# Fused attention and four-expert layer on one core: the second expert with seven half-size products in five pairs of token tiles instead of seven, and three vector operations moved

## The chip, the cores and the metric

The kernel runs on one core of one Trainium2 chip. The metric is the device time of one execution in microseconds (us). Before the change the median of three runs is 383.03 us (382.89 to 383.79). The profiled execution, from which all the lines of the profile come, has a span of 381.7 us. The engines are named as the profile names them: PE is the matrix engine (PEld its weight loads), DVE the vector engine, ACT the scalar engine, POOL and SP the two that mostly issue transfers.

## What is computed

The first half is attention for 4 batches, 8 heads, 768 positions and a head size of 64. Three of the heads look at all earlier positions, five only at 4 first positions and a window of 64. The result, seen as 3072 tokens of 512 values, goes through four dense experts whose outputs are added with the weights `p`:

```python
def _moe_ref(x, domain_probs, w1, w2):       # x: 3072 x 512
    p = domain_probs / (domain_probs.sum(-1, keepdims=True) + 1e-09)
    out = np.zeros((N, D))
    for e in range(E):                       # E = 4, hidden size 1024
        h = np.maximum(x @ w1[e], 0.0)
        out += p[:, e:e+1] * (h @ w2[e])
    return out
```

## The kernel before, in words

The 3072 tokens are 24 tiles of 128. The first four tiles go through the experts one expert after the other. The other twenty are taken as ten *pairs* of tiles, called here by the number of the first tile: pair 4, 6, 8 and so on to 22. Each pair is one call of `pair_steps(nt0, nxt)`, where `nxt` is the next pair.

**Layer one of a pair.** The token inputs of each expert are first multiplied by that expert's weight `p` (`scale_inputs`, L1111; one operation of 128x1024 elements, or two of 128x512 where the pair straddles two attention chunks). The products can then be added over the experts with no further scaling. An expert's first layer is done in one of two ways:

- `plain_layer1`: 32 matmuls with 256 columns (L1155) and four ReLUs on ACT (L1164);
- `winograd_layer1`: a Strassen-Winograd scheme with seven products of half size in each direction, which is 56 matmuls with 128 columns (L1184). It needs sums of the inputs (`scaled_sums`, L1125 and L969, and one more subtraction in place on the quarter `x_part(e, 0, 1)`), three copies to `kept` on ACT (L1194), three additions with ReLU on DVE (L1201) and one ReLU on ACT (L1234). It also needs sums of the weights, made once for each expert (`first_weight_sums`).

`EW = (3, 2)` names the experts that may be done in the second way. Expert 3 is done so in every pair. Expert 2 is done so only where `two(nt0)` holds, in the last `LAST` pairs. With `LAST = 7` these are pairs 10 to 22, and the weight sums of expert 2 are made in pair 8. A table called `order` in `pair_steps` says how the steps of the plain experts (`n`) and of the two others (`a` for expert 3, `b` for expert 2) follow each other and which DVE operation stands behind which group of steps.

**Layer two of a pair.** It is the same seven-product scheme over all four experts at once: seven products of 16 matmuls with 256 columns (L1287), in the order A11, A12, S2, S1, S3, S4, A22. The sums S2, S3 and S4 (each two halves of 128x1024 elements, L969) are made on DVE between them. Two accumulators in PSUM, `x` and `y`, are emptied by ACT copies (L1307) and DVE additions (L1310, `add`). Behind the products S3, S4 and A22 also stand the scalings and input sums of the *next* pair. If the next pair does expert 2 in the second way, the flag `ahead` holds, and the scalings of experts 3, 0 and 2 stand there. Otherwise only those of experts 0 and 3 do, and expert 2 is scaled in the middle of the next pair's layer one.

**Attention between the pairs.** Everything is issued by one program in a fixed order for each engine. The loop at the end draws a step from `moe_steps()`, adds its nominal time to `spent`, and puts in attention steps for a later chunk of tokens when `spent` has passed what `plan` gives. So each engine's queue holds a mixture: score products (L660) and value products (L714, L786) on PE, exponentials (L678) and the logarithm and exponential of a reciprocal (L804, L814) on ACT, mask products (L682), normalisation (L809, L739 to L743) and copies of keys (L290, L274) on DVE. The last three pairs have no attention beside them.

Of the kernel before, what the change touches and what calls it, by code (L numbers as in the profile page):

```python
# [19 lines left out]
def kernel(  # L20
# [80 lines left out]
    def bank():  # L101
        return pA.tile([P, 512], FP32, name="pA", bufs=4)
# [11 lines left out]
    EW = (E - 1, E - 2)  # L114
# [422 lines left out]
    def mm_ns(cols):  # L537
        return cols / 2.4 + 2.5
# [429 lines left out]
    def minus(out, a, b):  # L968
        nc.vector.tensor_tensor(out=out, in0=a, in1=b, op=ALU.subtract)  # L969
# [9 lines left out]
    def w1_part(e, j, k):  # L979
        c = e * DMP + j * KH  # L980
        return w1sb[:, c : c + KH, k * FN : (k + 1) * FN]
# [3 lines left out]
    def first_weight_sums(e):  # L985

        return [
            lambda: minus(t1[e, 0], w1_part(e, 0, 1), w1_part(e, 0, 0)),
            lambda: minus(t1[e, 1], w1_part(e, 1, 1), t1[e, 0]),
            lambda: minus(t1[e, 2], w1_part(e, 1, 0), t1[e, 1]),  # L990
            lambda: minus(w1_part(e, 0, 1), w1_part(e, 1, 1), w1_part(e, 0, 1)),
        ]
# [81 lines left out]
    def pieces(nt0):  # L1074

        g0, j0 = divmod(nt0, 3)
        n0 = min(3 - j0, PT)
        yield g0, j0 * P, 0, n0
        if n0 < PT:
            yield g0 + 1, 0, n0, PT - n0  # L1080
# [12 lines left out]
    def scaled(e):  # L1093
        if e in own_room:
            return own_room[e]
        n = 2 if e == EW[0] else e % 2
        x = xs_of[0][:, n * DMP * PC : (n + 1) * DMP * PC]
        return x.rearrange("p (c x) -> p c x", c=DMP)

    def scale_inputs(nt0, e):  # L1100

        if xs_of[0] is None:
            xs_of[0] = moe.tile([P, XS], FP16, name="xs", tag="xs", bufs=1)
        xs = scaled(e)
        for g, c0, t0, n in pieces(nt0):
            require(g)
            xin = xT[g][:, :, c0 : c0 + n * P].rearrange("p c (t x) -> p c t x", t=n)
            o = xs[:, :, t0 * P : (t0 + n) * P].rearrange("p c (t x) -> p c t x", t=n)
            pb = pB_of[nt0][:, t0 : t0 + n, e, :]
            pb = pb.rearrange("p t (c x) -> p c t x", c=1)  # L1110
            nc.vector.tensor_tensor(  # L1111
                out=o, in0=xin, in1=pb.to_broadcast([P, DMP, n, P]), op=ALU.mult
            )

    def x_part(e, i, j):
        return scaled(e)[:, j * KH : (j + 1) * KH, i * P : (i + 1) * P]

    def x_sum(n):

        n0 = WT * NSH * P + n * KH * P  # L1120
        return kSf[:, n0 : n0 + KH * P].rearrange("p (c x) -> p c x", c=KH)

    def scaled_sums(e):

        nc.vector.tensor_tensor(  # L1125
            out=x_sum(0), in0=x_part(e, 1, 0), in1=x_part(e, 1, 1), op=ALU.add
        )
        minus(x_sum(1), x_sum(0), x_part(e, 0, 0))
        minus(x_part(e, 1, 0), x_part(e, 0, 0), x_part(e, 1, 0))
# [9 lines left out]

    PSHARE = 1.57  # L1140

    LAST = 7

    def two(nt0):
        return nt0 >= pairs[-LAST]

    def pair_steps(nt0, nxt):
# [29 lines left out]
        def winograd_layer1(e, x, y):  # L1177

            ns = HT * KH * mm_ns(P)

            def product(ps, w, a, first):
                for f in range(HT):
                    for ct in range(KH):
                        nc.tensor.matmul(  # L1184
                            out=ps[:, f * P : (f + 1) * P],
                            lhsT=w[:, ct, f * P : (f + 1) * P],
                            rhs=a[:, ct, :],
                            start=(first and f == 0 and ct == 0),
                            stop=(ct == KH - 1),
                            skip_group_check=True,  # L1190
                        )

            def keep(n, ps):
                nc.scalar.copy(out=kept[n], in_=ps)  # L1194

            def block(n):
                return blocks[:, n, e * HT : (e + 1) * HT, :]

            def add(n, ps, b):

                nc.vector._custom_dve(  # L1201
                    TENSOR_ADD_SAT,
                    out=block(b),
                    in0=ps.rearrange("p (f x) -> p f x", f=HT),
                    in1=kept[n].rearrange("p (f x) -> p f x", f=HT),
                    s0=LARGEST,
                    s1=0.0,
                )

            def t(n):  # L1210
                return t1[e, n]

            product(x, w1_part(e, 0, 0), x_part(e, 0, 0), True)
            keep(0, x)
            yield ns, 0.5
            z = bank()
            product(z, w1_part(e, 1, 0), x_part(e, 0, 1), True)
            add(0, z, 0)
            yield ns, 0.5
            product(x, t(1), x_sum(1), False)  # L1220
            keep(1, x)
            yield ns, 0.5
            product(y, t(0), x_sum(0), True)
            keep(2, y)
            minus(x_part(e, 0, 1), x_part(e, 0, 1), x_sum(1))
            yield ns, 0.5
            product(x, w1_part(e, 0, 1), x_part(e, 1, 0), False)
            add(2, x, 3)
            yield ns, 0.5
            product(y, w1_part(e, 1, 1), x_part(e, 0, 1), False)  # L1230
            add(1, y, 2)
            yield ns, 0.5
            product(x, t(2), x_part(e, 1, 1), False)
            nc.scalar.activation(  # L1234
                out=block(1), in_=x.rearrange("p (f x) -> p f x", f=HT), func=AF.Relu
            )
            yield ns, 0.5

        a, b = (winograd_layer1(e, *y) for e, y in zip(EW, (banks, banks[::-1])))

        more = []
        if nt0 == pairs[-LAST - 1]:
            more = first_weight_sums(EW[1])
# [39 lines left out]
        def product(ps, a, b, first, middle=None):  # L1285
            for k in range(KT):
                nc.tensor.matmul(  # L1287
                    out=ps,
                    lhsT=a[:, k, :],
                    rhs=b(k),  # L1290
                    start=(first and k == 0),
                    stop=(k == KT - 1),
                    skip_group_check=not first,
                )
                if k == KT // 2 - 1:
                    if middle is not None:
                        middle()
                    yield KT // 2 * mm_ns(HN), PSHARE

        def b(k, n):  # L1300
            return lambda kt: whole_b(k, n, kt // HT, kt % HT)
# [4 lines left out]
        def keep(n, ps):  # L1306
            nc.scalar.copy(out=s[:, n, :], in_=ps)  # L1307

        def add(n, ps, i, j):
            nc.vector.tensor_tensor(  # L1310
                out=o[:, i, j * HN : (j + 1) * HN], in0=ps, in1=s[:, n, :], op=ALU.add
            )

        def store(i, j=None):
            r = slice((nt0 + i) * P, (nt0 + i + 1) * P)
            c = slice(0, DM) if j is None else slice(j * HN, (j + 1) * HN)
            nc.sync.dma_start(out=out[r, c], in_=o[:, i, c])

        def second_sum(n):
            k = slice(n * KT // 2, (n + 1) * KT // 2)  # L1320
            minus(S2[:, k, :], S1[:, k, :], A11[:, k, :])
# [11 lines left out]
        ahead = nxt and two(nxt)  # L1333
# [3 lines left out]
        yield from product(x, A11, b(0, 0), True)  # L1337
        keep(0, x)
        second_sum(0)
        yield half  # L1340
        yield from product(y, A12, b(1, 0), True, lambda: second_sum(1))
        add(0, y, 0, 0)
# [12 lines left out]
        add(2, x, 1, 1)  # L1355
        if last:
            keep(3, x)
        else:
            scale_inputs(nxt, 0)
        yield half  # L1360
        yield from product(
            y, S4, b(1, 1), False, lambda: scaled_sums(EW[0]) if ahead else None
        )
        add(1, y, 0, 1)
        if nxt is not None:
            scale_inputs(nxt, EW[1] if ahead else EW[0])
        store(0)
        if last:
            store(1, 1)
# [18 lines left out]
            return  # L1388
        yield from product(x, A22, t(2), False)
        nc.scalar.copy(out=o[:, 1, 0:HN], in_=x)  # L1390
        if not ahead:
            scaled_sums(EW[0])
        if more:
            more[3]()
# [91 lines left out]
    def require(a):  # L1486
        drained = False
        while state["a"] <= a:
            attention_step()
            drained = True  # L1490
        if drained:
            tick(LAG)
        while any(g <= a for _, _, g in behind):
            behind.pop(0)[1]()
# [48 lines left out]
```

The softmax here doesn't subtract the row's maximum and nothing guards it: scores larger than these inputs give would overflow.

## Time and profile before

| what | value |
|---|---|
| device time, median of 3 | 383.03 us |
| span of the profiled run | 381.7 us |
| PE busy | 368.1 us (96%), 4224 matmuls |
| DVE busy | 283.2 us (74%) |
| ACT busy | 227.6 us (60%) |
| POOL busy | 111.5 us (29%) |
| granted PE clock | 1.00 throughout |

The pairs begin at 88.3 us. The busy time of an engine is a sum of its records. A matmul's record runs from its start to its modelled end (272 ns for 256 columns), while the next one starts long before that. So PE counts as busy as long as one matmul follows another, and the time that PE loses shows as a small gap in that share. The `idle` bracket of a timeline line is the gap in front of it, with the engine and line whose event ended it. Since the record in front covers the latency of the last matmul, the true loss at such a place is about 0.16 us more than the bracket: 272 ns of a record less the 109 ns at which such matmuls follow each other.

### The profile page before, as it was taken

The numbers are of one execution on the slowest core, as the hardware profiler recorded it, in microseconds if no ns is written. First come the engines' busy times: TensorE is split into PE (matmuls) and PEld (weight loads), VectorE is DVE, ScalarE is ACT, GpSimd is POOL, SyncE is SP. The second block draws the span as 40 slices with busy tenths as digits, with TensorE's granted clock in tenths as the row PEclk, the third lists the DMA queues.
The fourth block names the chain that finished last, engine by engine and source line by source line (L and its number), as shares of the span: only waits on it lengthen the run. The fifth ranks groups of instructions, "written<-read, shape, count | busy, mean of one in ns | idle before, by whom it ended". The sixth has DMA issues, their size and how long they took to land.

```text
span 381.7 us, 10324 instructions
## 1 busy us (share of the span) xinstructions
PE 368.1 (96%) x4224; PEld 310.8 (81%) x4224; DVE 283.2 (74%) x617; ACT 227.6 (60%) x475; POOL 111.5 (29%) x154
## 2 busy tenths in 40 slices
PE   8889999999999999999999899799999999999996
PEld 4754466678998988998889798798998999998996
DVE  6774768797797689979679869957957956857562
ACT  3863479547776785775666756665677362360630
POOL 8925563961066048027302550210000000000000
PEclk9999999999999999999999999999999999999999
DMA  9999999999799299899906991961220110300101
GB/s 167 153 204 204 197 192 179 179 206 85 109 108 160 77 103 148 142 99 79 169 12 74 180 121 26 116 125 14 61 78 2 55 58 2 112 3 2 58 0 57
DMA packets 124772, 39.25 MB, mean 103 GB/s; under 512 B 113728, under 2 KB 118404, under 8 KB 124724
## 3 DMA queue, kind: packets, MB, share of 16 engines
q0 software_dynamic: 86848, 19.01, 58.8%
q1 hardware_dynamic: 36276, 19.18, 22.2%
q8 instruction: 33, 0.54, 0.6%
q10 hardware_dynamic: 1600, 0.39, 0.5%
q14 instruction: 15, 0.12, 0.1%
HBM read 44.89 MB, written 6.34 MB: 134 GB/s over the span
## 4 chain that ended last, share of the span: by engine, by line
PE 81%; DVE 12%; ACT 4%; issue 2%; DVEq 0%; ACTq 0%
PE pO L1287 25%; PE pA L1155 19%; PE pO L1184 10%; PE pA L1026 7%; PE pO L1047 7%; PE pA L660 4%; DVE xs L1111 2%; PE pA L1184 2%; PE pV L714 2%; ACT rc L804 2%; PE pV L786 1%; DVE xT L809 1%; DVE hA L969 1%; PE pO L430 1%; DVE es L682 1%
## 5 line engine op out<-in xcount | busy, mean ns | idle before, releaser
L1287 PEld LDWEIGHTS <-hA 128*128 128x128 f16 x1104 | 104.9, 98 | 13.7 <-issue 1.3
L1164 ACT ACTIVATE hA<-pA 128x512 f16<-128x512 f32 x92 | 55.0, 598 | 37.0 <-PE pA L1155 35.1
L1287 PE MATMUL pO<-w2sb,hA 128*128 128x256 f16 x640 | 76.7, 272 | 0.3 <-DVE hA L1201 0.2
L678 ACT ACTIVATE es<-pA 128x384 f16<-128x384 f32 (+2 forms) x122 | 59.0, 511 | 28.4 <-PE pA L660 24.0
L1155 PEld LDWEIGHTS <-w1sb 128*128 128x128 f16 x736 | 68.7, 98 | 6.9
L1155 PE MATMUL pA<-xs,w1sb 128*128 128x256 f16 x512 | 64.6, 273 | 0.0
L306 POOL DMA_DIRECT2D vS<-in_v_dram x30 | 29.6, 987 | 117.1 <-PE pV L786 113.5
L1287 PE MATMUL pO<-tsb,hA 128*128 128x256 f16 x464 | 56.8, 272 | 0.7 <-DVE o L1310 0.7
L1111 DVE TENSOR_TENSOR xs<-xT,pB 128x1024 f16<-128x1024 f16 (+1 forms) x43 | 40.8, 969 | 0.0
L969 DVE TENSOR_TENSOR hA<-hA 128x1024 f16<-128x1024 f16 x60 | 39.7, 685 | 0.4
L1184 PEld LDWEIGHTS <-w1sb 128*128 128x128 f16 x544 | 33.8, 98 | 5.5 <-issue 3.0
L1039 ACT ACTIVATE hA<-pA 128x384 f16<-128x384 f32 (+1 forms) x64 | 22.2, 385 | 19.8 <-PE pA L1026 19.6
L1184 PE MATMUL pO<-xs,w1sb 128*128 128x128 f16 x408 | 30.6, 219 | 3.3 <-DVE o L1310 1.1
L1026 PE MATMUL pA<-xT,w1sb 128*128 128x384 f16 (+1 forms) x256 | 30.9, 273 | 1.4 <-DVE xT L767 1.3
L1201 DVE CUSTOM_DVE_ANT_0 hA<-pO,s 128x512 f16<-128x512 f32 x34 | 23.1, 689 | 12.2 <-ACT s L1194 6.5
L1194 ACT COPY s<-pO 128x512 f32<-128x512 f32 x51 | 29.4, 588 | 4.0 <-PE pO L1184 2.7
L1047 PE MATMUL pO<-w2sb,hA 128*128 128x512 f16 x128 | 30.7, 379 | 0.0
L1155 PE MATMUL pA<-hA,w1sb 128*128 128x256 f16 x224 | 29.0, 273 | 0.0
L1026 PEld LDWEIGHTS <-w1sb 128*128 128x128 f16 x256 | 19.4, 98 | 10.2 <-issue 1.9
L1307 ACT COPY s<-pO 128x256 f32<-128x256 f32 x31 | 11.6, 373 | 26.5 <-PE pO L1287 19.3
L1184 PEld LDWEIGHTS <-t1sb 128*128 128x128 f16 x408 | 25.9, 98 | 1.1 <-issue 0.2
L804 ACT ACTIVATE rc<-pV,eps 64x384 f32<-64x384 f32 x37 | 21.3, 576 | 8.0 <-PE pV L786 7.4
(138 smaller groups left out, 526.8 us busy)
## 6 DMA issues: line engine op xcount, KB each, us to landing
pB<-p_rows SPq DMA_DIRECT2D x10, 512.0 KB
out_dram<-o SPq DMA_DIRECT2D x19, 256.0 KB
w1sb<-in_moe_w_dram POOLq DMA_DIRECT2D x8, 512.0 KB, 9.2
w2sb<-in_moe_w_dram POOLq DMA_DIRECT2D x4, 1024.0 KB, 12.2
vS<-in_v_dram POOLq DMA_DIRECT2D x30, 112.0 KB, 4.6
k_rows<-in_k_dram POOLq DMA_DIRECT2D x18, 128.0 KB, 5.1
q<-in_q_dram POOLq DMA_DIRECT2D x18, 128.0 KB, 6.2
vR<-in_v_dram POOLq DMA_DIRECT2D x24, 48.0 KB, 5.4
```

The costliest lines, as they stand in the source:

```text
L306: gp.dma_start(out=t[:, :, own_v(h)], in_=windows_of(v, b, h, c))
L678: nc.scalar.activation(out=es[:, 0:cols], in_=ps[:, 0:cols], func=AF.Exp, scale=SC)
L804: nc.scalar.activation(out=rc[r, :], in_=ps[o, 0:CH], func=AF.Ln, bias=eps[o, :])
L969: nc.vector.tensor_tensor(out=out, in0=a, in1=b, op=ALU.subtract)
L1026: nc.tensor.matmul(out=pss[ft][:, 0:cols_n], lhsT=w1sb[:, e * DMP + ct, ft * P : (ft + 1) * P], rhs=x[:, ct, :], start=(n == 0), stop=(n = ...
L1047: nc.tensor.matmul(out=ps_o, lhsT=hs[:, ft, j * P : (j + 1) * P], rhs=w2sb[:, e * FTP + ft, :], start=(ft == 0), stop=(ft == FTP - 1),)
L1111: nc.vector.tensor_tensor(out=o, in0=xin, in1=pb.to_broadcast([P, DMP, n, P]), op=ALU.mult)
L1155: nc.tensor.matmul(out=ps[:, f * PC : (f + 1) * PC], lhsT=w1sb[:, e * DMP + ct, (f0 + f) * P : (f0 + f + 1) * P], rhs=xs[:, ct, :], start= ...
L1164: nc.scalar.activation(out=blocks[:, b0 : b0 + 2, k0 : k0 + 2, :].rearrange("p t f x -> p f t x"), in_=ps.rearrange("p (f t x) -> p f t x" ...
L1184: nc.tensor.matmul(out=ps[:, f * P : (f + 1) * P], lhsT=w[:, ct, f * P : (f + 1) * P], rhs=a[:, ct, :], start=(first and f == 0 and ct == ...
L1194: nc.scalar.copy(out=kept[n], in_=ps)
L1287: nc.tensor.matmul(out=ps, lhsT=a[:, k, :], rhs=b(k), start=(first and k == 0), stop=(k == KT - 1), skip_group_check=not first,)
```

## The change

The change has four edits.

1. `LAST` goes from 7 to 5. Pairs 10 and 12 do expert 2 by `plain_layer1`, and the weight sums of expert 2 are made in pair 12 instead of pair 8.
2. In `winograd_layer1` the subtraction in place on `x_part(e, 0, 1)`, which the sixth product reads, stands directly behind the first addition and no longer behind the fourth product.
3. In layer two with `ahead`, the scaling of expert 0 for the next pair stands in the first product, between the two halves of S2, and no longer behind S3.
4. In layer two with `ahead`, the scaling of expert 2 stands behind the last product, no longer behind S4.

Edits 3 and 4 spread DVE operations over the products of layer two; edit 2 gives the sixth product its operand sooner.

```diff
-    LAST = 7
+    LAST = 5
...
             add(0, z, 0)
+            minus(x_part(e, 0, 1), x_part(e, 0, 1), x_sum(1))
             yield ns, 0.5
...
             keep(2, y)
-            minus(x_part(e, 0, 1), x_part(e, 0, 1), x_sum(1))
...
         second_sum(0)
+        if ahead:
+            scale_inputs(nxt, 0)
         yield half
...
         if last:
             keep(3, x)
-        else:
+        elif not ahead:
             scale_inputs(nxt, 0)
...
         add(1, y, 0, 1)
-        if nxt is not None:
-            scale_inputs(nxt, EW[1] if ahead else EW[0])
+        if nxt is not None and not ahead:
+            scale_inputs(nxt, EW[0])
         store(0)
...
         nc.scalar.copy(out=o[:, 1, 0:HN], in_=x)
-        if not ahead:
+        if ahead:
+            scale_inputs(nxt, EW[1])
+        else:
             scaled_sums(EW[0])
```

## The prediction

> **What bounds the kernel now.** I read the page first (PE busy 96%, so the question is the last 4%), then the busy time of each engine pair by pair, then the timeline of PE with only those lines that have an idle bracket, then the timeline of DVE at those places. The busy times by pair, the columns being span, then busy time and instruction count of PE, PEld, DVE, ACT and POOL:
>
> ```profile
> 88.30:119.00 30.70, 30.70 (x381) 27.75 (x380) 25.37 (x58) 22.42 (x46) 10.78 (x12) 1.00 0.99 101
> 119.00:149.80 30.80, 30.77 (x390) 27.72 (x389) 22.82 (x48) 22.42 (x45) 12.00 (x15) 1.00 1.27 114
> 149.80:183.60 33.80, 32.75 (x412) 29.78 (x410) 30.15 (x67) 22.82 (x46) 13.62 (x16) 1.00 1.05 123
> 183.60:216.60 33.00, 31.58 (x424) 28.39 (x424) 24.73 (x56) 23.34 (x46) 5.25 (x7) 1.00 0.80 94
> 216.60:246.00 29.40, 27.76 (x358) 25.33 (x359) 24.55 (x64) 17.50 (x36) 10.54 (x13) 1.00 1.02 96
> 246.00:273.10 27.10, 26.43 (x310) 23.48 (x309) 20.09 (x45) 16.95 (x33) 2.63 (x3) 1.00 0.36 65
> 302.60:328.10 25.50, 25.50 (x292) 23.51 (x290) 17.43 (x35) 10.33 (x21) 0.00 (x0) 1.00 0.13 44
> ```
>
> The reader sees that PE never pauses in pairs 4, 6 and 18 (first, second and last line). It loses 1.05 us in the stretch to 183.6, 1.42 in the next, 1.64 in the next and 0.67 in the next. In the first of these DVE is busy 30.15 of 33.80 us. The places, from PE's timeline (start, length, line, matmuls, and in brackets the idle time before and who ended it):
>
> ```profile
> 178.66 0.61 PE L1184 MATMUL pO<-xs,w1sb 128*128 128x128 f16 x8 [0.24 <-DVE o L1310]
> 183.66 0.62 PE L1184 MATMUL pO<-xs,w1sb 128*128 128x128 f16 x8 [0.86 <-DVE xs L969]
> 211.74 0.34 PE L786 MATMUL pV<-es,vS 128*128 128x48 f16 x7 [1.17 <-DVE xT L809]
> 216.67 0.62 PE L1184 MATMUL pO<-xs,w1sb 128*128 128x128 f16 x8 [0.21 <-DVE xs L969]
> 239.68 1.03 PE L1287 MATMUL pO<-tsb,hA 128*128 128x256 f16 x8 [0.67 <-DVE o L1310]
> 242.67 0.61 PE L1184 MATMUL pO<-xs,w1sb 128*128 128x128 f16 x8 [0.90 <-DVE o L1310]
> 247.70 0.61 PE L1184 MATMUL pO<-xs,w1sb 128*128 128x128 f16 x8 [0.53 <-ACT s L1194]
> ```
>
> Six of seven are released by DVE, and all lie where one pair ends and the next begins, where the scalings are crowded. With 0.16 us of hidden latency each they cost 0.40, 1.02, 1.33, 0.37, 0.83, 1.06 and 0.69 us: 5.70 us. A gap of 0.2 us at 213.7 has no bracket but shows in the start times. So PE is the bound, except at these boundaries, where DVE's queue is.
>
> **What the Trainium skill says.** "TensorE: Matmul & The Clock Gate", the section "Wait — 56ns, not 53.3ns?", prices a warm matmul at N/2.4 + 2.5 ns: 55.8 ns for 128 columns, 109.2 for 256. The chain of waits agrees (start, length, matmuls):
>
> ```profile
> 328.72 0.87 PE pA L1155 x8
> 329.60 0.89 PE pO L1184 x16
> ```
>
> That is 109 and 55.6 ns. The same page says of queues (Part 1, "Architectural detail") that DVE and ACT are strict FIFO; so an operation that PE needs waits for whatever stands before it, and moving a scaling is moving everything behind it. "VectorE: DVE Perf Modes" (the section on the perf-mode tier table) has a two-input operation at two elements a cycle for 16-bit data in SBUF and at one with any fp32 or PSUM operand. The trace agrees in kind: sums of 128x1024 f16 take 0.685 us, scalings of as many elements, with fp32 weights, 1.217 us. So a scaling is the dearest single thing in that queue.
>
> **The change part by part.**
>
> *Edit 1 on PE.* In pairs 10 and 12, 56 matmuls of 128 columns become 32 of 256: 56 x 55.6 = 3.11 us against 32 x 109 = 3.49 us. PE has 0.38 us more in each pair, 0.76 us in all. PE is the bound, so this is paid in full.
>
> *Edit 1 on DVE.* Each of these pairs loses three additions (3 x 0.69, L1201), four input operations (4 x 0.285, L1125 and L969) and two instructions of the S1 sum (4 x 0.42 become 2 x 0.69): 2.07 + 1.14 + 0.30 = 3.5 us. The four weight sums (4 x 0.68 = 2.7 us) go from pair 8, which has 30.15 us of DVE work, to pair 12, which has 24.55 and keeps 24.55 - 3.5 + 2.7 = 23.8. In pair 8 the scaling of expert 2 (1.22) and its place before the next pair go too. ACT is unchanged: three copies of 0.588 and one ReLU of 0.594 against four ReLUs of 0.598.
>
> *Which waits this ends.* Pair 10 then begins with three plain groups (2.6 us of PE) before its first half product. In the new instruction order the first half product therefore comes 2.6 us after the DVE addition that it waits for: 0.40 gone. The 1.02 us at 183.66 came from a subtraction that stood behind the weight sum, an addition and a scaling; here edit 2, the missing scaling and the missing sum all help: gone. The 0.37 at 216.67 is the same wait in pair 12: gone, with the 0.2 at 213.7. The value products at 211.74 wait for a normalisation (L809) that follows two additions, three scalings and the input sums in DVE's queue. In the new order one scaling and the sums are no longer before it. Counting from the end of product S4 at 208.35: addition 0.35, scaling 1.2, normalisation 0.5, so 210.85 at the latest, while PE is free at 210.45; of 1.33 us about 0.45 stays. Ended: 0.40 + 1.02 + 0.37 + 0.2 + 0.88 = 2.87 us.
>
> *Edits 3 and 4 at the end of pair 12.* The wait at 239.68 is for the addition behind S3. In the new order expert 0's scaling (2 x 0.64) stands before it, earlier in the queue, where DVE had an idle stretch of 1.03 us at 229.6; 0.3 to 0.4 us of delay remains. A mask product is now also just before it, which needs an exponential that ended at 239.54. So the addition starts at about 240.0, not 239.21, while PE is free 0.18 us later than before (value products were moved in front): the wait grows by about 0.45. Behind it, however, the scaling is gone: input sums 0.87, normalisation 0.55 and addition 0.42 end 1.8 us later, and PE needs 1.9 us for the last product and seven small matmuls. The wait of 1.06 at 242.67 ends. The 0.69 at 247.70 comes from ACT, where the two operations L804 and L814 now stand even before two copies: I keep it.
>
> *Edit 3 in pair 14.* This is the added wait. Between the halves of S2 now stands a scaling of 1.22 us; behind it are the second half of S2, a copy of keys and everything later. PE waits for that half in the middle of product S2. In the trace of before, DVE reached these sums late:
>
> ```profile
> 259.50 0.43 DVE L1133 TENSOR_TENSOR hA<-hA 128x512 f16<-128x512 f16 x1 [1.35 <-ACT hA L1234]
> 259.96 0.56 DVE L809 TENSOR_TENSOR xT<-pV,rc 64x384 f16<-64x384 f32 x1
> 260.56 1.29 DVE L969 TENSOR_TENSOR hA<-hA 128x1024 f16<-128x1024 f16 x2
> 261.31 2.79 PE L1287 MATMUL pO<-tsb,hA 128*128 128x256 f16 x24
> ```
>
> The first half ends at 261.2 and PE starts S2 at 261.31. With the scaling, the second half ends at 263.0, and PE wants it at 262.2: 0.9 us with the semaphore. In pairs 12 and 16 the same count leaves at least 0.7 us to spare, in the pairs without attention 0.7 us too (second half wanted at 345.3, ready at 344.5). There edits 2 to 4 cost nothing, because PE is never held: 25.5 us a pair is its own work (64 x 109 + 112 x 55.6 + 112 x 109 ns = 25.4).
>
> *Sum.* Ended 2.87 + 1.06 = 3.93; added 0.45 + 0.9 = 1.35; PE 0.76. Net 3.93 - 1.35 - 0.76 = 1.8 us. 383.03 - 1.8 = 381.2 us.
>
> **The rivals.**
>
> *No new waits form* (0.2). DVE enters pair 12 with less behind it, and ACT may release pair 14's S1 sum sooner, since the stalls that put it late go. Then 3.93 - 0.76 = 3.2 us are won: 379.9 us. For it: the added waits rest on differences of half a microsecond. Against: the L804 and L814 that delay the ReLU (L1234) stand in the new order just as before.
>
> *The waits only change places* (0.2). If the attention chain (exponential, mask product, value products) is what holds the boundary of pair 10, the 1.33 us stay, and pair 14's wait comes to 1.3 us. Then 3.93 - 0.88 - 0.45 - 1.3 - 0.76 = 0.5 us: 382.5 us, within what can be told from nothing. For it: masks wait 4.7 us in all for exponentials in pair 10. Against: the releaser named at 211.74 is the normalisation, and DVE is busy without a pause from 202.7 to 212.5.
>
> *Slower* (0.1). Only the 0.40 and 1.02 end, while the matmuls (0.76) are paid, pair 14 loses 1.3 us and the weight sums in pair 12 bring 1 us of the congestion of pair 8 with them: 1.42 - 0.76 - 1.3 - 1.0 = -1.6, so 384.7 us. Against: pair 12 has 4.9 us of room on DVE where pair 8 had 3.7, and in its layer one, where three of the four sums stand, it lost 3.5 us of other work.
>
> **How the numbers follow.** The main case has 0.5. Faster by over 0.3% (under 381.88) takes the main case and the first rival: 0.7. Within 0.3%: 0.2. Slower: 0.1. The range leaves out the slower case and about half a tenth at the fast end: 379.3 (all waits named end, those at 239.68 and 247.70 in part as well) to 382.9.
>
> **What would show it.** Right: half products x952 become x840 and plain ones x736 become x800; PE's brackets at the starts of pairs 10, 12 and 14 are gone but for one of about 0.3 before value products; a bracket of about 1.2 before the last product of pair 12; one of about 0.8 inside product S2 of pair 14, released by L969. Wrong: a DVE queue in pair 12 as full as pair 8's was, brackets in pairs 16 to 20 that had none, or pair 14's S2 undisturbed.

## The result, and the profile after

The changed kernel takes 380.5 us (380.28 to 380.54, 4 runs) against 382.96 us (382.82 to 383.79, 4 runs) of the kernel before: a ratio of 0.993 with a 95% interval of 0.9913 to 0.9947. The forecast was 381.2.

The head of the page after the change (busy time, share of the span, instructions):

```profile
span 378.3 us, 10207 instructions
PE 368.1 (97%) x4176; PEld 310.7 (82%) x4176; DVE 277.3 (73%) x599; ACT 227.4 (60%) x475; POOL 112.5 (30%) x154
```

PE has 48 matmuls fewer and DVE 5.9 us less work; ACT is the same. The busy times pair by pair, cut at the starts of the pairs (columns as in the prediction: span, then PE, PEld, DVE, ACT and POOL). First pairs 8, 10 and 12 of the kernel before:

```profile
149.63:178.66 29.03, 28.79 (x359) 26.15 (x357) 25.45 (x60) 20.08 (x41) 8.85 (x11) 1.00 0.95 111
178.66:211.92 33.26, 31.23 (x418) 28.22 (x417) 26.34 (x59) 22.19 (x44) 8.93 (x11) 1.00 0.85 95
211.92:242.67 30.75, 28.91 (x372) 26.07 (x368) 24.48 (x62) 19.41 (x38) 11.50 (x13) 1.00 1.00 108
```

Then pairs 8, 10, 12, 14 and 16 of the changed kernel:

```profile
149.07:177.69 28.62, 28.62 (x359) 26.15 (x357) 22.64 (x53) 19.85 (x40) 8.45 (x11) 1.00 0.90 110
177.69:209.21 31.52, 31.43 (x395) 28.24 (x393) 22.35 (x50) 22.22 (x43) 9.19 (x11) 1.00 0.86 97
209.21:238.92 29.71, 29.12 (x354) 26.34 (x350) 25.05 (x61) 19.42 (x39) 11.65 (x14) 1.00 1.11 114
238.92:269.95 31.03, 29.76 (x365) 26.45 (x361) 23.65 (x53) 19.38 (x38) 2.93 (x3) 1.00 0.46 77
269.95:298.84 28.89, 28.38 (x377) 25.89 (x375) 22.40 (x46) 18.56 (x37) 0.00 (x0) 1.00 0.12 34
```

Pair 8 has no pause left and pair 10 only 0.09 us (span against PE busy); before, they had 0.24 and 2.03. The pauses are now in pairs 12, 14 and 16 (0.59, 1.27 and 0.51 us; before 1.84, 0.67 and 0.70). PE's timeline names those over 0.1 us, with the idle time in front and who ended it in brackets:

```profile
236.49 0.34 PE L786 MATMUL pV<-es,vS 128*128 128x48 f16 x7 [0.42 <-DVE x_pair L743]
237.00 1.91 PE L1287 MATMUL pO<-tsb,hA 128*128 128x256 f16 x16 [0.17 <-DVE o L1310]
243.30 1.10 PE L1184 MATMUL pO<-xs,w1sb 128*128 128x128 f16 x16 [0.50 <-ACT s L1194]
258.91 1.92 PE L1287 MATMUL pO<-tsb,hA 128*128 128x256 f16 x16 [0.69 <-DVE hA L969]
283.46 0.61 PE L1184 MATMUL pO<-xs,w1sb 128*128 128x128 f16 x8 [0.50 <-ACT s L1194]
```

The two waits for ACT (L1194) stood in the kernel before too, at 247.70 and 286.73. The last but one is new: PE stops in the middle of product S2 of pair 14. DVE's timeline there shows why:

```profile
255.38 0.43 DVE L1133 TENSOR_TENSOR hA<-hA 128x512 f16<-128x512 f16 x1 [1.34 <-ACT hA L1234]
255.84 0.56 DVE L809 TENSOR_TENSOR xT<-pV,rc 64x384 f16<-64x384 f32 x1
256.43 0.69 DVE L969 TENSOR_TENSOR hA<-hA 128x1024 f16<-128x1024 f16 x1
257.04 1.22 DVE L1111 TENSOR_TENSOR xs<-xT,pB 128x1024 f16<-128x1024 f16 x1
258.17 0.68 DVE L969 TENSOR_TENSOR hA<-hA 128x1024 f16<-128x1024 f16 x1
```

The moved scaling (L1111) lies between the two halves of S2 (L969). The second half ends at 258.85, and PE's matmul starts at 258.91.

**A ruler for the experiments.** The start of a pair is the first layer-one matmul behind the last L1287 of the pair before, read from PE's timeline. The distance from one start to the next repeats closely: in all fourteen profiles pair 4 takes 30.48 or 30.49 us, pair 6 30.72 or 30.73, and pair 20 25.46 or 25.47. What differs from run to run is the time before pair 4, 87.68 to 88.84 us. So the lengths of pairs 8 to 16 resolve a tenth of a microsecond where the medians do not. Medians are given too. A median and these lengths differ by a few tenths, since the part in front is in the median. All the runs, in us:

| run | edits | pair 8 | 10 | 12 | 14 | 16 | sum | median |
|---|---|---|---|---|---|---|---|---|
| before | none, LAST 7 | 29.03 | 33.26 | 30.75 | 30.55 | 28.98 | 152.57 | 382.96 |
| after | 1 to 4, LAST 5 | 28.62 | 31.52 | 29.71 | 31.03 | 28.89 | 149.77 | 380.5 |
| e1_last_only | 1 | 28.62 | 31.52 | 30.50 | 30.17 | 28.75 | 149.56 | 380.48 |
| e2_moves_only | 2, 3, 4 | 28.61 | 30.91 | 29.79 | 31.42 | 29.06 | 149.79 | 380.23 |
| e3_scale0_back | 1, 2, 4 | 28.62 | 31.52 | 30.51 | 30.16 | 28.75 | 149.56 | 380.09 |
| e4_scale0_later | 1, 2, 4, and 3 one product later | 28.62 | 31.52 | 30.73 | 30.17 | 29.33 | 150.37 | 381.0 |
| e5_minus_only | 2 | 29.02 | 32.60 | 30.36 | 30.55 | 28.97 | 151.50 | 382.03 |
| e6_scalings_only | 3, 4 | 28.62 | 31.49 | 30.17 | 31.41 | 29.05 | 150.74 | 381.09 |
| e7_split5 | 1, 2, 4, and 3 in pair 12 only | 28.62 | 31.53 | 29.72 | 30.16 | 28.75 | 148.78 | 379.39 |
| e8_split7 | 2, 4, and 3 up to pair 12, LAST 7 | 28.62 | 30.90 | 29.79 | 30.55 | 28.97 | 148.83 | 379.3 |
| e9_scale2_only | 4 | 29.02 | 32.40 | 31.05 | 30.55 | 28.98 | 152.00 | 382.48 |
| e10_last2 | 2 to 4, LAST 2 | 28.62 | 31.53 | 28.80 | 29.55 | 28.28 | 146.78 | 377.61 |
| e11_last3 | 2 to 4, LAST 3 | 28.61 | 31.53 | 28.81 | 29.54 | 28.28 | 146.77 | 377.7 |
| e12_last3_only | LAST 3 alone | 28.62 | 31.53 | 28.80 | 29.54 | 28.29 | 146.78 | 377.62 |

The kernel before, run again beside the later groups, had medians of 382.96, 382.96, 383.05 and 383.08 us.

One caution for the columns of pairs 12 and 14. `LAST` also shifts attention: with `LAST = 7` a group of seven score products (L660) starts in pair 14 (at 243.11 us in the kernel before), in all the runs with a lower `LAST` it starts in pair 12 (at 238.74 in the changed kernel). PE is held by it for 0.18 us. Between runs of unlike `LAST`, pair 12 is longer and pair 14 shorter by that much for this reason alone. The sums are not touched.

### The profile page after: what moved, and what is told of

Same layout as the page of the kernel before. It is cut to its first block, busy times and chain, and to the rows that moved or that the text cites. A ratio compares the mean times of both kernels' runs of the same rounds, so it can differ in the third digit from the quotient of the medians.

```text
span 378.3 us, 10207 instructions
## 1 busy us (share of the span) xinstructions
PE 368.1 (97%) x4176; PEld 310.7 (82%) x4176; DVE 277.3 (73%) x599; ACT 227.4 (60%) x475; POOL 112.5 (30%) x154
## 4 chain that ended last, share of the span: by engine, by line
PE 89%; DVE 6%; ACT 3%; issue 1%; DVEq 0%; ACTq 0%
PE pO L1287 28%; PE pA L1155 23%; PE pO L1184 10%; PE pA L1026 7%; PE pO L1047 7%; PE pA L660 5%; PE pV L714 2%; PE pV L786 2%; PE pA L1184 2%; DVE xs L1111 1%; ACT rc L804 1%; PE pO L430 1%; DVE hA L969 1%; PE pA L558 1%; DVE es L682 1%
## 5 line engine op out<-in xcount | busy, mean ns | idle before, releaser
L1287 PEld LDWEIGHTS <-hA 128*128 128x128 f16 x1104 | 104.8, 98 | 13.9 <-DVE hA L969 1.0
L1164 ACT ACTIVATE hA<-pA 128x512 f16<-128x512 f32 x100 | 59.6, 598 | 36.6 <-PE pA L1155 34.9
L1155 PEld LDWEIGHTS <-w1sb 128*128 128x128 f16 x800 | 74.9, 98 | 7.8
L1155 PE MATMUL pA<-xs,w1sb 128*128 128x256 f16 x640 | 80.6, 273 | 0.0
L1287 PE MATMUL pO<-w2sb,hA 128*128 128x256 f16 x640 | 76.8, 272 | 0.1
L1287 PE MATMUL pO<-tsb,hA 128*128 128x256 f16 x464 | 56.7, 273 | 0.9 <-DVE hA L969 0.7
L1111 DVE TENSOR_TENSOR xs<-xT,pB 128x1024 f16<-128x1024 f16 (+1 forms) x45 | 43.3, 981 | 0.0
L969 DVE TENSOR_TENSOR hA<-hA 128x1024 f16<-128x1024 f16 x60 | 39.7, 685 | 0.3
L1184 PEld LDWEIGHTS <-w1sb 128*128 128x128 f16 x480 | 30.0, 98 | 2.3 <-issue 1.4
L1201 DVE CUSTOM_DVE_ANT_0 hA<-pO,s 128x512 f16<-128x512 f32 x30 | 20.2, 688 | 11.0 <-ACT s L1194 5.4
L1026 PEld LDWEIGHTS <-w1sb 128*128 128x128 f16 x256 | 19.4, 98 | 10.2 <-issue 1.9
L1184 PE MATMUL pO<-xs,w1sb 128*128 128x128 f16 x360 | 26.7, 219 | 1.0 <-ACT s L1194 1.0
L809 DVE TENSOR_TENSOR xT<-pV,rc 64x384 f16<-64x384 f32 x37 | 20.5, 554 | 9.4 <-ACT rc L814 7.0
L1194 ACT COPY s<-pO 128x512 f32<-128x512 f32 x45 | 26.0, 588 | 1.4 <-PE pO L1184 0.9
L682 DVE TENSOR_TENSOR es<-es,mS 128x384 f16<-128x384 f16 (+1 forms) x40 | 13.7, 344 | 13.5 <-ACT es L678 13.4
```

The costliest lines, as they stand in the source:

```text
L1026: nc.tensor.matmul(out=pss[ft][:, 0:cols_n], lhsT=w1sb[:, e * DMP + ct, ft * P : (ft + 1) * P], rhs=x[:, ct, :], start=(n == 0), stop=(n = ...
L1111: nc.vector.tensor_tensor(out=o, in0=xin, in1=pb.to_broadcast([P, DMP, n, P]), op=ALU.mult)
L1155: nc.tensor.matmul(out=ps[:, f * PC : (f + 1) * PC], lhsT=w1sb[:, e * DMP + ct, (f0 + f) * P : (f0 + f + 1) * P], rhs=xs[:, ct, :], start= ...
L1164: nc.scalar.activation(out=blocks[:, b0 : b0 + 2, k0 : k0 + 2, :].rearrange("p t f x -> p f t x"), in_=ps.rearrange("p (f t x) -> p f t x" ...
L1184: nc.tensor.matmul(out=ps[:, f * P : (f + 1) * P], lhsT=w[:, ct, f * P : (f + 1) * P], rhs=a[:, ct, :], start=(first and f == 0 and ct == ...
L1287: nc.tensor.matmul(out=ps, lhsT=a[:, k, :], rhs=b(k), start=(first and k == 0), stop=(k == KT - 1), skip_group_check=not first,)
```

## Experiments

**Which edit made the time: edit 1 alone, and the other three alone.**

```diff
# e1_last_only, against the kernel before
-    LAST = 7
+    LAST = 5
# e2_moves_only, against the changed kernel
-    LAST = 5
+    LAST = 7
```

> Only edit 1 (LAST = 5), the three operations where they were. Theory A, order in DVE's queue: the waits at the starts of pairs 10 and 12 end as in the changed kernel, the two waits before and after the last product of pair 12 stay (0.83 and 1.06 us), product S2 of pair 14 has no wait; about 380.6 us. Theory B, load alone (only the missing DVE work of edit 1 counts, and edits 2 to 4 do nothing but bring the wait in S2): 379.6 us. Theory C, the moves alone win: 383.7 us, since only the dearer matmuls (0.76) are left.

> Edits 2 to 4 with LAST = 7. Theory A: the subtraction made sooner ends the waits of 1.02 us in pair 10 and 0.37 in pair 12, the moved scalings end most of 0.40 before pair 10 and 1.06 before pair 14, S2 of pair 14 waits 0.87, and the scaling in the first product may cost up to 0.9 in the crowded layer two of pairs 8 and 10; no matmuls are added: 381.0 us (380.4 to 381.9). Theory B, load alone: 383.8. Theory C, the moves alone win: 380.5 or less.

Each half alone wins as much as the whole: 380.48 us (ratio 0.9936, 0.9921 to 0.9952) and 380.23 us (0.993, 0.9915 to 0.9945). Over pairs 8 to 16 they win 3.01 and 2.78 us, and together 2.80. Theory B falls by the second run (383.8 forecast) and theory C by the first (383.7 forecast). Theory A has the first number. The second lies under its range, where C had put it: the cost of up to 0.9 us that A allowed for the scaling in pairs 8 and 10 did not come. So the edits are substitutes: the waits at both ends of pair 10 end, wholly or for the most part, when DVE's order alone is changed (e2_moves_only) and when edit 1 takes work from it. Edit 1 changes the order too, since pairs 10 and 12 then follow the other `order` table, so its run does not separate load from order. Load alone is not what counts: in pair 12 DVE's work goes up from 24.48 to 24.79 us in e1_last_only, and the pair is 0.25 us shorter. Behind edit 1, the other three cost 0.21 us. Where, the columns of the table tell: they win 0.79 us in pair 12 (30.50 to 29.71) and lose 0.86 in pair 14 and 0.14 in pair 16.

**Edit 3 undone.**

```diff
# e3_scale0_back, against the changed kernel
         second_sum(0)
-        if ahead:
-            scale_inputs(nxt, 0)
...
-        elif not ahead:
+        else:
             scale_inputs(nxt, 0)
```

> The changed kernel with expert 0's scaling back behind S3 (edit 3 undone). Theory A: the 0.87 us in S2 of pair 14 end, and about 1.0 comes back at the end of pair 12, where the addition behind S4 stands again behind a scaling: 380.6 us (380.2 to 381.0). Theory B, the place of this scaling counts for nothing but the wait that it makes in S2: 379.6 us.

Every pair is within 0.01 us of e1_last_only. The wait in S2 of pair 14 is gone (31.03 to 30.16), and the wait for the addition behind S4 is back at the end of pair 12:

```profile
239.54 0.61 PE L1184 MATMUL pO<-xs,w1sb 128*128 128x128 f16 x8 [0.63 <-DVE o L1310]
```

The waits are as theory A has them; the second one cost 0.79 us where 1.0 was expected, and the median of 380.09 lies 0.1 under its range. This run says more. It differs from e1_last_only by edits 2 and 4, and these are worth nothing at all once `LAST` is 5.

**The same scaling one product later.**

```diff
# e4_scale0_later, against e3_scale0_back
         add(0, y, 0, 0)
+        if ahead:
+            scale_inputs(nxt, 0)
         yield half
```

> The changed kernel with expert 0's scaling one product later, behind the second half of S2 and the addition of the second product. Theory A: DVE then has two products (3.5 us) before PE wants S3, so the 0.87 us in S2 of pair 14 end and nothing takes their place: 379.6 us (379.4 to 379.9). Rival, the wait only moves to S3 or to the first accumulator's release: 380.5 us.

Theory A's number was missed by 1.4 us: 381.0 us, slower than the changed kernel. The wait in pair 14 did end (30.17), but pair 12 went to 30.73, and pair 16 to 29.33, where value products now wait for a normalisation (0.31 us in brackets at 292.44). The rival was right that a wait moves, though not to the place that it named. I had counted only when PE wants S3, and not the mask products (L682) that stand behind the scaling in the same queue. DVE's timeline of this run, and then PE's:

```profile
232.98 0.68 DVE L969 TENSOR_TENSOR hA<-hA 128x1024 f16<-128x1024 f16 x1
233.58 0.22 DVE L682 TENSOR_TENSOR es<-es,mC 128x128 f16<-128x128 f16 x1
```

```profile
233.85 0.24 PE L714 MATMUL pV<-vR,es 128*128 128x65 f16 x2 [0.74 <-DVE es L682]
```

DVE was busy all but without a pause from 226.9 us to the end of this mask at 233.80, with the scaling at 227.52, and value products of the attention waited 0.74 us for it. A scaling has no idle room there. In front of this stretch, where the changed kernel has it, DVE is idle for 0.94 us in e3_scale0_back.

**Edit 2 alone, and edits 3 and 4 without it, at LAST = 7.**

```diff
# e5_minus_only, against the kernel before
             add(0, z, 0)
+            minus(x_part(e, 0, 1), x_part(e, 0, 1), x_sum(1))
...
             keep(2, y)
-            minus(x_part(e, 0, 1), x_part(e, 0, 1), x_sum(1))
# e6_scalings_only: the changed kernel with these lines back and LAST = 7
```

> The kernel before with edit 2 alone (the subtraction directly behind the first addition). Theory A: pair 10 loses its wait of 1.02 us (33.26 to about 32.2 us) and pair 12 that of 0.37 (30.75 to about 30.4), nothing else moves: 381.6 us. Rival, the subtraction is only the last of a row of late operations, and PE then waits for the next one: 382.9 us.

> LAST = 7 with edits 3 and 4 (the scalings moved), the subtraction where it was. Theory A, edits are substitutes: a scaling less before the first addition already brings the subtraction in time, so the pairs are as with all three moves (28.6, 30.9, 29.8, 31.4, 29.1 us): 380.2 us. Rival, each edit ends its own wait: 1.02 and 0.37 come back, 381.6 us.

Alone, edit 2 is worth 0.66 us in pair 10 and 0.39 in pair 12 (382.03 us, ratio 0.9974). The 0.66 is less than the 1.02 of the wait (a bracket of 0.86 and the hidden 0.16), since an ACT copy now ends the wait instead:

```profile
182.72 0.61 PE L1184 MATMUL pO<-xs,w1sb 128*128 128x128 f16 x8 [0.20 <-ACT s L1194]
```

That is 0.20 + 0.16 us. Without edit 2 the scalings leave 0.41 us to the subtraction in pair 10 and 0.21 in pair 12, so pairs 10 and 12 are 0.58 and 0.38 longer than with it (e2_moves_only). Theory A's guess, that edit 2 is spare beside edits 3 and 4, is wrong at LAST = 7, and so is the rival's, that its whole 1.39 us comes back: 0.96 does. Edit 2 is spare only beside edit 1.

**Edit 4 alone.**

```diff
# e9_scale2_only, against the kernel before
-        if nxt is not None:
-            scale_inputs(nxt, EW[1] if ahead else EW[0])
+        if nxt is not None and not ahead:
+            scale_inputs(nxt, EW[0])
...
-        if not ahead:
+        if ahead:
+            scale_inputs(nxt, EW[1])
+        else:
             scaled_sums(EW[0])
```

> The kernel before (LAST = 7) with edit 4 alone: expert 2's scaling behind the last product. Theory A: in DVE's queue the normalisation that the value products at the end of pair 10 wait for now stands before that scaling, not behind it, so the 1.33 us shrink to about 0.1 to 0.4; the waits on the addition behind S4 (0.40, 1.06) and on the subtraction (1.02, 0.37) stay, since nothing before them is moved: sum over pairs 8 to 16 about 151.5 us, 381.8 us. Rival, these value products wait for the attention chain (rc on ACT), not for the queue: 382.9 us.

The bracket of 1.17 us before the value products of pair 10 is down to 0.03, and pair 10 is 0.86 us shorter. So these products did wait for the queue, and the rival falls. But the scaling now lies in front of the first addition of the next pair. The subtraction in pair 10 waits 1.13 us instead of 0.86, and in pair 12 a bracket for an ACT copy grows from 0.06 to 0.36 and the pair by 0.30. The sum is 152.00: half a microsecond won of the one expected.

**The better place, pair by pair.**

```diff
# e7_split5, against the changed kernel; e8_split7: LAST = 7 and the condition nt0 <= 12
-        if ahead:
+        early = ahead and not two(nt0)
+        if early:
             scale_inputs(nxt, 0)
...
-        elif not ahead:
+        elif not early:
             scale_inputs(nxt, 0)
```

> The changed kernel with edit 3 only in pair 12, whose layer one has no second half-product expert; in pairs 14 to 20 expert 0's scaling stands behind S3 as before. Theory A, the best place differs by pair: pair 12 keeps 29.7 us, pair 14 goes from 31.03 to 30.17, pair 16 to 28.75: about 1.0 us less than the changed kernel, 379.5 us. Rival, what one pair gains the next gives back: 380.3 us.

> LAST = 7 with edits 2 and 4 everywhere and edit 3 only up to pair 12. Theory A: as the run with all moves and LAST = 7, but pair 14 loses the wait in S2 (31.42 to about 30.5 us): 379.3 us. It tells whether half products in pairs 10 and 12 are worth keeping once DVE's queue is in order: theory A says yes by about 0.2 us; rival (the half products overload DVE in any order): 380.2 us or more.

Both came out at the expected number, 379.39 and 379.3 us (ratios 0.9904 and 0.9901). The lengths of the pairs add up as the single runs said: 29.72 of the changed kernel in pair 12 with 30.16 and 28.75 of e3_scale0_back. But the sums 148.78 and 148.83 say that half products in pairs 10 and 12 are then worth as much as plain ones. Pair 10 gains 0.63 us by them, and pairs 12, 14 and 16 lose 0.07, 0.39 and 0.22 (for equal attention 0.25, 0.21 and 0.22). The 0.2 us that theory A gave the half products there is not seen.

**Fewer half products beside attention.**

```diff
# e10_last2 and e11_last3, against the changed kernel; e12_last3_only, against the kernel before
-    LAST = 5
+    LAST = 2
# and 3, and 3
```

> The changed kernel with LAST = 2: pairs 14, 16 and 18 too do expert 2 by plain products. Theory A: pair 18, which has no waits, shows the bare price of plain products, 25.46 to 25.84 us; pair 14 loses the wait in S2 (0.87) and some of its 0.67, and pays 0.38; pair 16 pays 0.38 less about 0.6 of waits. Sum of the three 0.2 to 0.8 us under the changed kernel: 379.9 us. Rival, the plain form is the better one everywhere beside attention and costs nothing in pair 18 (weight loads hide the difference): under 379.5 us.

> The changed kernel with LAST = 3: plain products for expert 2 in every pair beside attention, half products in the three pairs without it. Theory A: as LAST = 2, but pair 18 gets its 0.37 us back (25.46), and pair 16 takes the weight sums (2.7 us of DVE work) without a wait: 377.2 us. Rival, the weight sums make pair 16 wait: 377.6 us or more.

> The kernel before with LAST = 3 alone, no operation moved. Theory A: without half products of expert 2 beside attention no DVE order matters any more, so edits 2 to 4 are worth nothing: 377.2 us, pairs within 0.1 us of those of the run with the moves. Rival, the moves are still worth what they were worth in pair 12 of the changed kernel (0.8 us): 378.0 us.

This is the largest step, and theory A had sized it too low for LAST = 2: 377.61, 377.7 and 377.62 us (ratios 0.9863, 0.9858 and 0.9857, the last with an interval of 0.9841 to 0.9873). Pair 18, whose busy times in e10_last2 are

```profile
295.71:321.54 25.83, 25.83 (x266) 23.47 (x264) 17.36 (x34) 10.58 (x20) 0.00 (x0) 1.00 0.12 42
321.54:347.01 25.47, 25.47 (x291) 23.48 (x289) 17.50 (x34) 10.34 (x20) 0.00 (x0) 1.00 0.13 44
```

with plain products in pair 18 (first line) and half products in pair 20, shows the bare price: 25.83 - 25.46 = 0.37 us. So the rival, which had the better number for LAST = 2, has the wrong reason: plain products do cost something in pair 18. In pairs 14 and 16 of these runs PE pays that price and is still 1.49 and 0.61 us faster than in the changed kernel. Of the 1.49, though, 0.87 is the wait that edit 3 had brought into S2. Without any moves, e1_last_only against e12_last3_only, the gain is 0.63 and 0.46 us. In e11_last3, pairs 10 to 16, a pause is left in pair 10 alone:

```profile
177.96:209.49 31.53, 31.44 (x395) 28.23 (x393) 22.37 (x50) 22.24 (x43) 9.20 (x11) 1.00 0.87 99
209.49:238.30 28.81, 28.81 (x355) 26.19 (x351) 21.41 (x52) 19.41 (x39) 11.65 (x14) 1.00 1.09 111
238.30:267.84 29.54, 29.54 (x341) 26.59 (x337) 20.92 (x46) 19.50 (x38) 2.93 (x3) 1.00 0.53 84
267.84:296.12 28.28, 28.28 (x352) 25.83 (x351) 22.67 (x44) 18.82 (x37) 0.00 (x0) 1.00 0.13 37
```

The waits that end with the half products in pairs 14 and 16 are for ACT more than for DVE. At 243.30 PE waits for a copy to `kept` before the next product may write into the same accumulator, and in ACT's queue the logarithm and the exponential of attention stand in front of two copies (changed kernel):

```profile
241.51 0.57 ACT L804 ACTIVATE rc<-pV,eps 64x384 f32<-64x384 f32 x1
242.12 0.52 ACT L814 ACTIVATE rc<-rc 64x384 f32<-64x384 f32 x1
242.66 1.07 ACT L1194 COPY s<-pO 128x512 f32<-128x512 f32 x2
```

At 283.46 in pair 16 it is the same. With the hidden 0.16 us these two waits are 0.66 and 0.67 us.

What I had missed is that pair 12 gains too (29.71 to 28.80), although its own layer one is the same. With pair 14 plain, `ahead` no longer holds in pair 12: the weight sums and the scaling of expert 2 leave it, DVE's work falls from 25.05 to 21.41 us, and the scaling of expert 3 stands behind S4 instead of in the middle of S3. The traces say which of these counts. In the changed kernel the three weight sums of layer one end at 220.5, and after one more sum DVE is idle for 2.68 us before 223.82; the fourth sum (240.32) and the scaling of expert 2 (239.12) start after PE's last wait in this pair (237.00). What stands in the queue just before the operations that PE waits for is the scaling of expert 3. The changed kernel:

```profile
234.17 1.28 DVE L1111 TENSOR_TENSOR xs<-xT,pB 128x512 f16<-128x512 f16 x2
236.53 0.42 DVE L1310 TENSOR_TENSOR o<-pO,s 128x256 f32<-128x256 f32 x1
```

and e11_last3, where the next scaling is that of expert 0 and comes behind the addition:

```profile
235.61 0.42 DVE L1310 TENSOR_TENSOR o<-pO,s 128x256 f32<-128x256 f32 x1
235.95 1.28 DVE L1111 TENSOR_TENSOR xs<-xT,pB 128x512 f16<-128x512 f16 x2
```

Counted from the start of the pair, the addition (L1310) comes 1.2 us sooner. So it is again the order, as far as these two traces show it; no run moves this scaling alone.

Without moves all pairs are the same to 0.01 us, as theory A had it for e12_last3_only, and the rival (378.0) falls. That the weight sums make no wait is seen from pair 16, which takes them in e11_last3 and not in e10_last2 and has 28.28 us in both; the rival of e11_last3 (377.6 or more) met the number and not the reason. Between LAST = 2 and 3 the medians show nothing, though pair 18 differs by 0.36 us; in the two profiled runs the one with LAST = 2 began pair 4 earlier by 0.42 us (87.72 against 88.14), which hides it.

## Why the prediction was right

The time lies in the range and the mechanism held: waits for DVE where pairs meet end, and the price on PE and a new wait in S2 of pair 14 eat part of it. The gain was larger, 2.46 us of the median (2.80 over pairs 8 to 16) against 1.8. Step by step:

- **Price on PE.** 0.38 us a pair forecast; 0.37 measured in pair 18 of e10_last2.
- **Waits at the starts of pairs 10 and 12.** All forecast gone, all gone. Pair 8 is 0.41 us shorter (0.40 forecast). That it was edit 1 and not edit 2 that did it, the forecast left open ("edit 2, the missing scaling and the missing sum all help"); e1_last_only shows that edit 1 is enough.
- **Value products at the end of pair 10.** About 0.45 us was to stay. In the timeline they start at 209.03, the eight matmuls before them having started at 207.91 and taken 0.87: 0.25 us stayed. Mis-sized by 0.2.
- **DVE's work.** The forecast's table is not cut where pairs start: 183.60, 216.60 and 246.00 lie 3 to 5 us behind the starts of pairs 10, 12 and 14. Pair 8 had 25.45 us of DVE work and not 30.15; the rest belongs to the start of pair 10. In pair 12 the work was to fall to 23.8, and it rose from 24.48 to 25.05. That is nearly as much as pair 8 had, which the forecast had named as a sign of being wrong. The time fell all the same, so the load of a pair was not the measure to go by.
- **End of pair 12.** The wait at 239.68 was to grow from 0.83 by 0.45 to 1.28. It became two, 0.42 and 0.17 in brackets. Counted as the gap between the end of the small matmuls' own work and the next start, the first is 0.6 and the second 0.3, together 0.9. The bracket of about 1.2 that was to show is not there. Mis-sized by 0.4; the wait of 1.06 behind it ended as forecast.
- **S2 of pair 14.** 0.9 forecast; PE's first eight matmuls start at 257.17 and would end at 258.04, the rest start at 258.91: 0.87. e3_scale0_back, without edit 3, confirms it by 0.87 (31.03 to 30.16).
- **The wait for ACT at 247.70** was kept at 0.69 and stayed at 0.66 (0.50 and 0.16). Another one in pair 14, before the matmul at 254.26, is not in the forecast's list: the eight matmuls in front of it start at 253.60, so 0.66 us pass for 0.45 us of work, and 0.2 are lost. It is gone in the changed kernel.
- **No cost in pairs 16 to 20.** The forecast's tables leave pair 16 out, so its pauses of 0.70 us do not appear in them, nor in its 5.70. Right for pairs 18 and 20. In pair 16 edit 3 costs 0.14 (e1_last_only against the changed kernel); in the forecast's comparison with the kernel before that does not show, since the pair fell from 28.98 to 28.89.

The terms that were off, 0.2 for the value products, 0.4 at the end of pair 12, 0.2 for the unlisted wait and 0.1 in pair 16, are about the 1.0 us between 1.8 and 2.80. All of them lie on the same side.

Edits 3 and 4, by the forecast's own terms, were a loss: 1.06 - 0.45 - 0.9 = -0.3 us. The runs give -0.21. Three of the four edits of this change did nothing or slightly worse beside the first. The forecast had the number and did not draw the conclusion.

The rival "no new waits form" gave 379.9, as near as the main case, but not for its reason: the waits did form. The rival in which the waits change places falls, since 0.25 of the 1.33 us at the end of pair 10 stayed and S2 of pair 14 waits 0.87 and not 1.3. The rival in which the weight sums bring pair 8's congestion to pair 12 falls too: pair 12 became 1.04 us shorter. Waits that change places are real all the same: e4_scale0_later and e9_scale2_only show them.

Not settled: whether half products in pairs 14 and 16 would pay if ACT's copies did not stand behind attention's operations, and LAST = 4; no run has either.

## What to carry to other kernels

A scheme that saves matmuls and costs vector work has a price that depends on what runs beside it. Here it saves 0.37 us in pair 18, which has no attention beside it. In pairs 14 and 16 it loses 0.6 and 0.5 us without any moves, since attention's operations stand in the queues of the vector engine and of ACT in front of those that its products need. So the place to switch it on is, in this kernel, where the other work ends: LAST = 3, one number, is worth more than all four edits (377.6 against 380.5 us).

When several edits aim at the same waits, take them singly before adding them: gains of 3.01 and 2.78 us made 2.80 together. And before moving an operation earlier or later, list everything in that queue behind the new place and who waits for it, not only the consumer for whose sake it is moved.

## What the runs showed of the hardware

A stretch that PE bounds repeats to 0.01 us from run to run and from kernel to kernel (pair 20: 25.46 or 25.47 us in fourteen profiles). In the profiled runs the variation comes from before pair 4, a part which ends between 87.68 and 88.84 us.
